# Values of eight key tiles behind every second section, units of 2 heads by 1024 queries, and tables for the places of scores and maxima

## The chip, the core and the metric

The kernel runs on one NeuronCore of a Trainium2 chip. The metric is the device time of one execution in microseconds (us). TensorE is called PE in the profile, VectorE DVE, ScalarE ACT, GpSimd POOL, and SyncE, which issues the DMAs here, SP. PEld is TensorE's weight load.

## The reference

One sequence of 2048 tokens of width 576. The output is the input plus an attention branch times a gated feed-forward branch, both of the layer-normed input:

```python
x = A_x                                  # (1, 2048, 576), float32
xn = _layernorm(x)
q, k, v = heads(xn @ wqkv)               # 32 heads of 18
p = softmax(q @ k.T * 18 ** -0.5)
s = (p @ v) @ wo
y = (gelu(xn @ w_gate) * (xn @ w_up)) @ w_down     # inner width 4608
return x + s * silu(y)
```

(heads() stands for the reshape and transpose of the original.)

## The kernel before

**Three phases.** A prologue norms x, projects it to q, k and v and writes them to DRAM. An epilogue projects the attention's output by wo and combines the branches. Between them lies the long middle, in which attention and the feed-forward part are interleaved; the change is there.

**Feed-forward.** The 2048 tokens are four blocks of 512 (`NB`), the inner width 4608 is 18 rounds of two groups of 128 (`NR`, `G`). One block and one group make a **section**, 144 in all: 27 pairs of matmuls (line 437), each pair two products of 64 rows of the contraction side by side, into one PSUM tile `pgu` that holds the gate and the up product (128x512 each). Each fp32 operand is split into a high and a low part (`wh`, `wl`), and three of the four products are taken, so a section is 9 chunks by 3 terms. Its 16th pair (index `SWAP` = 15) waits until the one before it is through, because the two halves change places there. After a section ScalarE takes the gelu of the gate (L452) and VectorE multiplies by the up part (L455). GpSimd then forms sums of the halves (`sums_a`, L472 to L477) and splits them (`cut_a`, L461 to L464) for the **down products** (`py`, L538), which come after every second section (`downs`): seven products by a fast scheme instead of eight, added into M by VectorE (L585). The w_down side of that scheme (T) is formed in the core for 18 rounds (`FORMED`: 13 of the first block, 5 of the second): GpSimd makes sums (`sums_b`), ScalarE writes the high parts (`high_b`, L511 to L514), GpSimd the low parts (`low_b`), and the result is stored. Other rounds load T from there in four pieces (`t_piece`).

**Attention.** It works in units (`NU` = 32) of four heads by 512 queries. Each unit sees 2048 keys as four chunks (`NA`) of 512. For a unit there are 32 score products `pe` (L901; 128 keys by 512 queries, two heads at once), whose exponentials ScalarE writes to SBUF as `pT` (L902), and 32 products `pm` (L860), the same scores the other way round, 128 queries by 512 keys, of which VectorE takes the largest (`mx`, L861). The maxima run 40 products ahead of the scores, so that each unit's maxima are known when its scores are made: `max_parts` reduces them (`neg`, L869), transposes (`mt`, L872), and writes a high and a low part (`mhl`, L874 on ScalarE, L875 on GpSimd), which DMAs put into two rows of the query tile. The product of keys and queries then has the maximum already subtracted. The **values stage** is the product of `pT` and the value tiles VS (`acc`, L918): for each of four key tiles and each of four heads 128 keys by 512 queries into 32 rows, in fp32. The first stage of a unit copies the result to `accs` (L922, ScalarE), later ones add to it (L924, VectorE).

**How they are woven.** The order of TensorE and of SP's queue is written out by hand, while a scheduler orders ScalarE, VectorE and GpSimd, except where `keep_in_program_order` holds two instructions. Eleven sections lead (`FIRST` gives how many maxima products each holds), then come 128 attention sections, then five in the epilogue (`ENDS`). An attention section carries eight scores and eight maxima, in turn (`SLOTS`). `spread` decides where they stand among the 27 pairs: by the formula i * 27 // 16 + 1, with the two nearest to SWAP moved to it. It also runs hooks at given pairs, such as the splits of the next weights. Behind each attention section come the values of its four key tiles, `max_parts` if a unit's maxima are complete, down products after every second one, and `finish`, which hands out the sums, the splits and the hooks of the next section.

All products of the middle take PSUM tiles of 128x1024 fp32 from one ring of four (`ring`). `pgu` holds its tile from the first pair of its section until gelu and multiplication have read it; a `pe` or `pm` tile comes free when its exponential or its reduction has read it. Tiles are taken in TensorE's order.

A key tile KA is held as two planes of 512 keys, one for each two of the four heads, seven chunks deep (`KB`).

Of the kernel before, what the change touches and what calls it, by code (L numbers as in the profile page):

```python
# [8 lines left out]
F32 = mybir.dt.float32  # L9
# [12 lines left out]
KT = 4  # L22
# [6 lines left out]
VW = QD * (DH + 1)  # L29
NQ = H // QD  # L30
NU = NQ * NB
# [3 lines left out]
VC = NT // NA  # L35
KB, VB = 7, 2
# [4 lines left out]
FIRST = (0, 0, 4, 5, 4, 5, 4, 5, 5, 4, 4)  # L41
# [4 lines left out]
SWAP = 3 * NK  # L46
DC, TH = D // 2, TB // 2
# [4 lines left out]
OTS = (4, 9, 0, 5)  # L52
# [37 lines left out]
def kernel(ctx: ExitStack, tc: tile.TileContext, x, wqkv, wo, w_gate, w_up, w_down, out):  # L90
# [11 lines left out]
    oT = dram.tile([NQ, P, S], F32, name="oT")  # L102
    rT = dram.tile([H, S], F32, name="rT")
# [297 lines left out]
    FF = {"w": ahead, "xd": XD, "down": [], "gates": [], "n": 0, "hooks": {}, "raw": {},  # L401
# [3 lines left out]
    KA = ffn.tile([P, 2 * KB, TB], F32R, name="KA")  # L405
    KS = [[KA[:, 2 * i + r] for r in range(2)] for i in range(KB)]
# [17 lines left out]
    def gate_up():  # L424
# [21 lines left out]
        return [lambda i=i: pair(i) for i in range(len(terms))], pg, pu  # L446

    def activate(pg, pu, g, n):

        h = ffn.tile([P, 3 + 3 * g, TH], F32, name=f"h{g}", bufs=2 - g)  # L450
        t1 = h[:, 0:2].rearrange("p a t -> p (a t)")
        nc.scalar.activation(t1, pg, AF.Gelu_apprx_tanh)  # L452
# [120 lines left out]
    def down(b, r, then={}):  # L573
# [16 lines left out]
        if FF["n"] < NF - ENDS:  # L590
# [35 lines left out]
    def section(specials=(), slots=False):  # L626
# [6 lines left out]
        pairs, pg, pu = gate_up()  # L633
        hooks, FF["hooks"] = FF["hooks"], {}
# [14 lines left out]
        if g == 0 and (b, r) in FORMED:  # L649
            raw = FF["rawd"]  # L650
            hook(12, lambda: sums_b(raw))
# [5 lines left out]
        for p in spread(pairs, specials, 1 if slots else None, hooks):  # L657
            p()
# [5 lines left out]
        FF["act"] = activate(pg, pu, g, n)  # L664
# [9 lines left out]

    def finish():
# [3 lines left out]
        g, h, s = n % G, FF["act"], part(b, r)  # L679
        pool, vec, act = nc.gpsimd, nc.vector, nc.scalar  # L680
        keep = tc.keep_in_program_order

        def hook(i, what):
            FF["hooks"].setdefault(i, []).append(what)

        parts = FF.pop("parts", False)

# [570 lines left out]
```

## Time and profile before

| | before |
|---|---|
| time, median of 3 runs | 2540.55 us (2539.89 to 2540.68) |
| the profiled execution's own time | 2539.57 us |
| its span in the profile | 2537.8 us |
| granted TensorE clock, mean | 0.999 |
| gate and up products (L437) | 36% of the chain that ended last |
| values (L918), down products (L538) | 18%, 16% |
| maxima, scores (L860, L901) | 10%, 9% |

The chain that ended last is followed back from the last instruction: at each step to what released it, or to the instruction before it on its engine. A group of instructions is given by line, engine and operation, what it writes and reads, the count, the busy time in all and the mean of one in ns, then the engine's idle time just before them and what ended most of it. A timeline row has the start from the span's begin, the time to the end, engine, line, operation, the tiles, and in brackets a wait and what ended it; rows of one kind that follow each other are drawn together, with their count. TensorE's matmuls are pipelined, so that durations overlap, and starts tell more than ends.

### The profile page before, as it was taken

The numbers are of one execution on the slowest core, as the hardware profiler recorded it, in microseconds if no ns is written. First come the engines' busy times: TensorE is split into PE (matmuls) and PEld (weight loads), VectorE is DVE, ScalarE is ACT, GpSimd is POOL, SyncE is SP. The second block draws the span as 40 slices with busy tenths as digits, with TensorE's granted clock in tenths as the row PEclk, the third lists the DMA queues.
The fourth block names the chain that finished last, engine by engine and source line by source line (L and its number), as shares of the span: only waits on it lengthen the run. The fifth ranks groups of instructions, "written<-read, shape, count | busy, mean of one in ns | idle before, by whom it ended". The sixth has DMA issues, their size and how long they took to land.

```text
span 2537.8 us, 59061 instructions
## 1 busy us (share of the span) xinstructions
PE 2529.8 (100%) x23434; PEld 1837.8 (72%) x23434; DVE 1891.7 (75%) x2085; ACT 1652.5 (65%) x1889; POOL 1587.1 (63%) x1652
## 2 busy tenths in 40 slices
PE   9999999999999999999999999999999999999999
PEld 8888866666766667666667766677666677666789
DVE  5326788888888888888887888888887788888247
ACT  3223377777777776666777666667777776777721
POOL 3005688787787775666657556566667565566772
PEclk9999999999999999999999999999999999999999
DMA  8855455555575556655666666656557666665666
GB/s 265 291 190 140 119 172 170 157 159 169 168 219 151 163 175 162 155 166 163 170 188 186 171 175 164 170 168 170 155 159 204 170 170 168 173 168 146 189 208 219
DMA packets 417419, 447.04 MB, mean 176 GB/s; under 512 B 114292, under 2 KB 294260, under 8 KB 417144
## 3 DMA queue, kind: packets, MB, share of 16 engines
q1 hardware_dynamic: 417144, 443.27, 60.3%
q8 instruction: 186, 3.05, 0.5%
q14 instruction: 89, 0.73, 0.1%
HBM read 345.99 MB, written 97.13 MB: 175 GB/s over the span
## 4 chain that ended last, share of the span: by engine, by line
PE 99%; DVE 1%; issue 0%; DMA 0%; ACT 0%; DVEq 0%
PE pgu L437 36%; PE acc L918 18%; PE py L538 16%; PE pm L860 10%; PE pe L901 9%; PE po L198 7%; PE po L1072 2%; PE py L598 1%; PE pt L268 0%; DVE ol L1055 0%; DMA xx<-in_A_x_dram 0%; DVE bs L227 0%; DVE xx L1088 0%; DVE yy L1062 0%; DVE M L1211 0%
## 5 line engine op out<-in xcount | busy, mean ns | idle before, releaser
L902 ACT ACTIVATE pT<-pe 128x1024 f32<-128x1024 f32 x1024 | 1034.8, 1026 | 490.6 <-PE pe L901 463.8
L861 DVE TENSOR_REDUCE mx<-pm 128x2 f32<-128x1024 f32 x1024 | 1219.5, 1226 | 155.2 <-PE pm L860 144.7
L437 PE MATMUL pgu<-xd,wh 64*128 64x512 f32 x5184 | 984.5, 393 | 0.4
L437 PEld LDWEIGHTS pgu<-xd,wh 64*128 64x128 f32 x5184 | 508.4, 184 | 126.4 <-issue 28.2
L120 POOL TENSOR_SCALAR wh<-raw 128x384 fp32r<-128x384 f32 x402 | 203.3, 517 | 598.7 <-PE pgu L437 487.7
L437 PE MATMUL pgu<-xd,wl 64*128 64x512 f32 x2592 | 519.4, 389 | 0.0
L918 PE MATMUL acc<-pT,VS 128*32 128x512 f32 x4096 | 466.0, 595 | 0.0
L860 PE MATMUL pm<-KA,QT 64*128 64x512 f32 x2048 | 424.3, 402 | 0.3 <-DVE mx L861 0.2
L901 PE MATMUL pe<-QT,KA 64*128 64x512 f32 x2048 | 413.6, 391 | 0.0
L122 POOL TENSOR_TENSOR wl<-raw,wh 128x384 fp32r<-128x384 f32 x402 | 402.7, 1016 | 12.1
L538 PE MATMUL py<-T,ah 64*128 64x288 f32 x3848 | 389.8, 294 | 0.0
L585 DVE TENSOR_TENSOR M<-py,M 128x576 f32<-128x576 f32 x448 | 333.3, 756 | 55.6 <-PE py L538 40.0
L538 PEld LDWEIGHTS py<-T,ah 64*128 64x128 f32 x3848 | 315.8, 184 | 53.2 <-issue 52.8
L464 POOL TENSOR_TENSOR al<-h,ah 128x512 fp32r<-128x512 f32 (+1 forms) x143 | 295.4, 2066 | 49.2 <-ACT ah L461 38.2
L918 PEld LDWEIGHTS acc<-pT,VS 128*32 128x32 f32 x4096 | 120.0, 109 | 276.8 <-issue 229.8
L538 PE MATMUL py<-T,al 64*128 64x288 f32 x1924 | 293.0, 291 | 0.0
L437 PEld LDWEIGHTS pgu<-xd,wl 64*128 64x128 f32 x2592 | 253.9, 185 | 37.0 <-POOL wl L127 0.3
L860 PEld LDWEIGHTS pm<-KA,QT 64*128 64x128 f32 x2048 | 201.4, 184 | 86.1 <-ACT pT L902 48.3
L901 PEld LDWEIGHTS pe<-QT,KA 64*128 64x128 f32 x2048 | 194.4, 184 | 86.7 <-DVE mx L861 12.6
L455 DVE TENSOR_TENSOR h<-h,pgu 128x512 f32<-128x512 f32 x139 | 95.6, 688 | 193.4 <-ACT h L452 188.6
L538 PEld LDWEIGHTS py<-T,al 64*128 64x128 f32 x1924 | 190.3, 185 | 0.0
L452 ACT ACT_TABLE_LOAD x129 | 165.5, 1283 | 2.3
(151 smaller groups left out, 2140.9 us busy)
## 6 DMA issues: line engine op xcount, KB each, us to landing
T<-ts SPq DMA_DIRECT2D x98, 576.0 KB
KA<-qk SPq DMA_DIRECT2D x768, 72.0 KB
T<-ts SPq DMA_DIRECT2D x98, 432.0 KB
raw<-in_B_w_up_dram SPq DMA_DIRECT2D x288, 128.0 KB
raw<-in_B_w_gate_dram SPq DMA_DIRECT2D x144, 160.0 KB
ts<-T SPq DMA_DIRECT2D x36, 576.0 KB
VS<-vs SPq DMA_DIRECT2D x128, 152.0 KB
qk<-t SPq DMA_DIRECT2D x72, 256.0 KB
```

Of the source, the lines that this page charges most:

```text
L120: first = nc.gpsimd.tensor_scalar(hi, raw, 1.0, 1.0, op0=ALU.mult, op1=ALU.mult)
L122: keep(nc.gpsimd.tensor_tensor(lo, raw, f(hi), op=ALU.subtract))
L198: nc.tensor.matmul(o, st, m, start=(i == 0), stop=(i == len(terms) - 1))
L437: one = nc.tensor.matmul((pg, pu)[half ^ x], w[1 + wp][c // XG][rr, c % XG, :], xd[k][xp][rr, :], start=(i == 0), stop=(i == len(terms) - 1))
L464: low = two.tensor_tensor(lo, raw, f(hi), op=ALU.subtract)
L538: one = nc.tensor.matmul(py[:, t, 0:DC], h[rr, a, t * P:(t + 1) * P], T[rr, w, k], start=x == 0 and n == 0, stop=x == 1 and n == len(terms ...
L585: nc.vector.tensor_tensor(M[:, m], py[:, :, 0:DC], M[:, m], op=ALU.add)
L860: nc.tensor.matmul(pm[:, a], QS[u, r][rr, t * P:(t + 1) * P], KS[(u * NA + c) % KB][r][rr, :], start=True, stop=True)
L861: nc.vector.tensor_reduce(MX[u][:, 2 * r:2 * r + 2, t, c], pm, axis=AX.X, op=ALU.max)
L901: nc.tensor.matmul(pe[:, a], KS[(u * NA + c) % KB][r][rr, t * P:(t + 1) * P], QS[u, r][rr, :], start=True, stop=True)
L902: nc.scalar.activation(PT[u, kt][:, 2 * r:2 * r + 2, :], pe, AF.Exp, scale=SCALE)
L918: nc.tensor.matmul(ACC[u][32 * a:32 * a + 32, :], VS[(u * NA + c) % VB][:, v:v + 32], pt[:, a, :], start=first, stop=last, skip_group_chec ...
```

## The change

**Units.** A unit is two heads by 1024 queries instead of four heads by 512. Both have four planes of 512 (head by query half); the counts of products and of sections stay. All planes now use the same two heads of a key chunk, so that KA has one plane per chunk, and a VS tile holds two heads. K and V loads have half the bytes; the query tile is loaded as two heads by 1024 columns.

**Values.** The values of eight key tiles (`RUN`) come behind every second section, just ahead of the down products, and `pT` has eight buffers. So two attention sections follow each other without anything between them on TensorE. A unit is copied once and added once to `accs` (lines 926 and 928 after).

**Gelu.** The first section of a round (g = 0) does not take a gelu: ScalarE copies both halves of `pgu` into `h0`. After the second section both gelus run, with one change of tables, then both multiplications. `sums_a` and `cut_a` of both sections follow in one `finish` of the round.

**Places.** `spread` takes the places of the specials of the two sections of a round from a table, `PLACES`, the first row for the first section. The index says before which of the 27 pairs a special stands.

**Formed rounds.** `high_b(0)` stays behind the values, `high_b(1)` is hooked to pair 8 of the next section, and the other hooks move.

**Ends.** Ten sections lead instead of eleven and six end instead of five; one more section, with its down product, stands behind the attention, and the attention's output is loaded into a tile of its own (OO).

```diff
-VW = QD * (DH + 1)
-NQ = H // QD
-NU = NQ * NB
+VW = 2 * (DH + 1)
+NQ = H // 2
+NU = NQ * S // (2 * TB)
...
+RUN = 2 * VC
...
-FIRST = (0, 0, 4, 5, 4, 5, 4, 5, 5, 4, 4)
+FIRST = (0, 0, 5, 5, 5, 5, 5, 5, 5, 5)
...
+PLACES = ((1, 2, 4, 5, 7, 8, 10, 11, 13, 15, 15, 17, 19, 20, 22, 23), (4, 5, 6, 8, 9, 11, 12, 13, 15, 15, 17, 18, 20, 22, 24, 25))
...
-    at = [-(-(i + 1) * n // m) - 1 if first is None else i * n // m + first for i in range(m)]
-    for i in sorted(range(m), key=lambda i: abs(at[i] - SWAP + 0.1))[:2]:
+    at = PLACES[first] if first is not None and m == 2 * SLOTS else [-(-(i + 1) * n // m) - 1 if first is None else i * n // m + first for i in range(m)]
+    for i in () if at in PLACES else sorted(range(m), key=lambda i: abs(at[i] - SWAP + 0.1))[:2]:
...
-    KA = ffn.tile([P, 2 * KB, TB], F32R, name="KA")
-    KS = [[KA[:, 2 * i + r] for r in range(2)] for i in range(KB)]
+    KA = ffn.tile([P, KB, TB], F32R, name="KA")
+    KS = [KA[:, i] for i in range(KB)]
...
+        if n in ATT and g == 0:
+            sums = bass.AP(h.tensor, h.offset, [list(h.ap[0]), [3 * TH, 2], [1, TB]])
+            keep(nc.scalar.activation(sums, two, AF.Copy))
+            return h
         if n in ATT:
-            tc.keep_in_program_order(nc.scalar.activation(one_exp[:, 1:2], one_exp[:, 0:1], AF.Exp))
+            keep(nc.scalar.activation(t1, pg, gelu))
+            h0 = FF["act"]
+            keep(nc.scalar.activation(flat(h0, 0), flat(h0, 0), gelu))
+            keep(nc.scalar.activation(one_exp[:, 1:2], one_exp[:, 0:1], AF.Exp))
+            nc.vector.tensor_tensor(t1, t1, pu, op=ALU.mult)
+            nc.vector.tensor_tensor(flat(h0, 0), flat(h0, 0), flat(h0, 3), op=ALU.mult)
+            return h0, h
+        nc.scalar.activation(t1, pg, gelu)
...
-        for p in spread(pairs, specials, 1 if slots else None, hooks):
+        for p in spread(pairs, specials, g if slots else None, hooks):
...
+        if (b, r + 1) in FORMED:
+            hook(15, lambda: load_rawd(part(b, r + 1)))
+        if (b, r) in FORMED:
+            high_b(0)
+            hook(8, lambda: high_b(1))
+            hook(2, lambda: low_b(0))
+            hook(11, lambda: low_b(1))
+            for k, i in enumerate((13, 20)):
+                hook(i, lambda k=k: t_piece(s, k, True))
+            for k, i in enumerate((2, 9)):
+                hook(i, lambda k=k: t_piece(s, 2 + k, True), True)
+        else:
+            t_piece(s, 0)
+            for k, i in ((1, 5), (2, 13), (3, 21)):
+                if n + 1 == ATT.stop:
+                    t_piece(s, k)
                 else:
-                    high_b(0)
-                    high_b(1)
-                hook(9 if lead else 2, lambda: low_b(0))
-                hook(16 if lead else 10, lambda: low_b(1))
-                for k, i in enumerate((19, 24) if lead else (1, 3) if late else (13, 20)):
-                    hook(i, lambda k=k: t_piece(s, k, True))
-                sums_a(g, h, vec if lead else pool)
-                hook(12, lambda: cut_a(0, h, pool, pool, keep))
-            else:
-                for k, i in enumerate((2, 9)):
-                    hook(i, lambda k=k: t_piece(s, 2 + k, True))
-                behind(lambda k: (sums_a(g, h, pool, k), cut_a(1, h, pool, pool, keep)))
-        else:
-            if g == 0:
-                for k, i in enumerate((None, 5, 27, 27) if late else (None, 5, 13, 21)):
-                    if i is None:
-                        t_piece(s, k)
-                    else:
-                        hook(i, lambda k=k: t_piece(s, k))
-            behind(lambda k: (sums_a(g, h, pool, k), cut_a(g, h, pool, pool, k)))
-        if g == G - 1:
-            FF["down"].append((b, r, n + 1))
+                    hook(i, lambda k=k: t_piece(s, k))
+        k = keep if FF.pop("parts", False) or (n + 1) % (NR * G) == 0 else lambda i: i
+        h0, h1 = FF["act"]
+        sums_a(0, h0, pool)
+        sums_a(1, h1, pool, k)
+        cut_a(0, h0, pool, pool, k)
+        cut_a(1, h1, pool, pool, k)
+        FF["down"].append((b, r, n + 1))
...
-                nc.tensor.matmul(pm[:, a], QS[u, r][rr, t * P:(t + 1) * P], KS[(u * NA + c) % KB][r][rr, :], start=True, stop=True)
+                nc.tensor.matmul(pm[:, a], QS[u, r][rr, t * P:(t + 1) * P], KS[(u * NA + c) % KB][rr, :], start=True, stop=True)
...
-                PT[u, kt] = att.tile([P, QD, TB], F32, name="pT", bufs=4)
+                PT[u, kt] = att.tile([P, QD, TB], F32, name="pT", tag="pT", bufs=RUN)
...
-            first, last = kt % VC == 0, kt % VC == VC - 1
+            first, last = kt % RUN == 0, kt % RUN == RUN - 1
...
-                v = t * VW + (DH + 1) * a
+                v = t * VW + (DH + 1) * (a % 2)
...
-            if last and kt < VC:
+            if last and kt < RUN:
...
-            for kt in range(i * SLOTS // 2, (i + 1) * SLOTS // 2):
-                values(u, kt)
             if im == 0 and um <= NU:
                 max_parts(um - 1)
-            load_v(n + 2)
+            if i % 2:
+                for kt in range((i - 1) * VC, (i + 1) * VC):
+                    values(u, kt)
+                load_v(n + 1)
+                load_v(n + 2)
             tasks(n, 1)
-            downs()
+            if i % 2:
+                downs()
             tasks(n, 2)
-            finish()
-            for b in range(2):
-                if n == NU * NA - NA + 2 * b:
-                    load_o(b)
+            if i % 2:
+                finish()
...
+        load_raw(FF["n"] + 2)
+        h, gelu = last_section()
+        todo.pop("rec")[0]()
+        down(NB - 1, NR - 4)
+        gelu()
+        for i in range(len(PIECES)):
+            t_piece(NR - 3, i)
+        sums_a(0, h, pool)
+        cut_a(0, h, pool, pool)
```

**The order.** The first place is TensorE around the end of a mid-kernel attention section. The numbers behind `xd` tell the section's operands; `pgu<-xd` are gate and up products, `pm<-KA,QT` maxima, `pe<-QT,KA` scores, `acc` values. Before, rows of the end of a first section, its values, and the start of the next:

```order
L437 MATMUL pgu<-xd_2_9475,wh 128x512 x2
L901 MATMUL pe<-QT_1963,KA 128x512 x2
L437 MATMUL pgu<-xd_3_9499,wh 128x512 x2
L437 MATMUL pgu<-xd_3_9499,wl 128x512 x2
L860 MATMUL pm<-KA,QT_1964 128x512 x2
L437 MATMUL pgu<-xd_3_9501,wh 128x512 x2
L918 MATMUL acc<-pT,VS_1937 32x512 x16
L437 MATMUL pgu<-xd_0_17946,wh 128x512 x2
L901 MATMUL pe<-QT_1963,KA 128x512 x2
L437 MATMUL pgu<-xd_0_17946,wl 128x512 x2
L860 MATMUL pm<-KA,QT_1964 128x512 x2
```

After, the same place on TensorE, the end of the first section of a round and the start of its second:

```order
L865 MATMUL pm<-KA,QT_1966 128x512 x2
L439 MATMUL pgu<-xd_2_17896,wh 128x512 x2
L439 MATMUL pgu<-xd_3_17922,wh 128x512 x2
L439 MATMUL pgu<-xd_3_17922,wl 128x512 x2
L439 MATMUL pgu<-xd_3_17924,wh 128x512 x2
L439 MATMUL pgu<-xd_0_17861,wh 128x512 x2
L439 MATMUL pgu<-xd_0_17861,wl 128x512 x2
L439 MATMUL pgu<-xd_0_17863,wh 128x512 x2
L439 MATMUL pgu<-xd_1_17876,wh 128x512 x2
L906 MATMUL pe<-QT_1965,KA 128x512 x2
L439 MATMUL pgu<-xd_1_17876,wl 128x512 x2
L865 MATMUL pm<-KA,QT_1967 128x512 x2
```

The last maxima product now stands five steps ahead of the border and not two, the values between the sections are gone, and the next section's first score stands behind four gate and up pairs instead of one.

The second place is TensorE within the second section of a round, where a maxima product's PSUM tile is needed again by the third special behind it. After (the first row is the section's first maxima product, the last the score that takes its tile):

```order
L865 MATMUL pm<-KA,QT_1967 128x512 x2
L439 MATMUL pgu<-xd_1_17878,wh 128x512 x2
L906 MATMUL pe<-QT_1965,KA 128x512 x2
L439 MATMUL pgu<-xd_2_17894,wh 128x512 x2
L439 MATMUL pgu<-xd_2_17894,wl 128x512 x2
L865 MATMUL pm<-KA,QT_1967 128x512 x2
L439 MATMUL pgu<-xd_2_17896,wh 128x512 x2
L906 MATMUL pe<-QT_1965,KA 128x512 x2
```

From the one to the other are seven pairs. By the formula of before the distance from a maxima product to that score is eight or nine pairs.

The third place is ScalarE around the end of a section in a round in which a unit's maxima are complete. `h` is the gelu's tile, `one_exp` a small exponential that calls the exponential's table back, `mhl` the maxima's high part. Before:

```order
L902 ACTIVATE pT<-pe 128x1024 x8
L452 ACT_TABLE_LOAD
L452 ACTIVATE h_18484<-pgu 128x512
L454 ACT_TABLE_LOAD
L454 ACTIVATE one_exp<-one_exp 128x1
L902 ACTIVATE pT<-pe 128x1024
L874 ACTIVATE mhl<-mt 128x32
L902 ACTIVATE pT<-pe 128x1024 x7
```

After, the same engine from the values of one round over both sections of the next (the second of three rows of `h` is the copy of both halves):

```order
L926 ACTIVATE accs<-acc 128x512
L907 ACTIVATE pT<-pe 128x1024 x8
L879 ACTIVATE mhl<-mt 128x32
L463 ACTIVATE h_18228<-pgu 128x2x512
L907 ACTIVATE pT<-pe 128x1024 x8
L466 ACT_TABLE_LOAD
L466 ACTIVATE h_18391<-pgu 128x512
L468 ACTIVATE h_18228<-h_18228 128x512
L469 ACT_TABLE_LOAD
L469 ACTIVATE one_exp<-one_exp 128x1
```

`mhl` moved from behind the next section's first exponential to ahead of the copy that empties `pgu`, and the gelu with its tables to behind the second section. In the formed rounds the three copies of `high_b`, in a row ahead of a section's eight exponentials before, are now one ahead of them and two behind the third.

More of the change, by code (lines that the diff above doesn't have):

```diff
@@ L571, in down_plain, with down @@
         halved(jobs)
-    def down(b, r, then={}):
+    def down(b, r, then={}, pairs=True):
         if b == 0 and r < PLAIN:
@@ L673, in downs, with lead_finish @@
             down(*FF["down"].pop(0)[:-1], then)
+    def lead_finish():
+        n = FF["n"] - 1
+        r, g = divmod(n, G)
+        if g == 1 and (0, r + 1) in NEXT:
+            load_rawd(r + 1)
+        if g == 0 and r > 0:
+            raw = FF["rawd"]
+            FF["hooks"].setdefault(4, []).append(lambda: cut_plain_b(raw))
+        cut_plain(g, FF["act"])
+        if g == G - 1:
+            FF["down"].append((0, r, n + 1))
     def finish():
@@ L972 @@
             downs()
-            finish()
+            lead_finish()
         scaled = gated = 0
@@ L1150 @@
         load_wo()
+        for b in range(2):
+            load_o(b)
         h, gelu = last_section()
-        todo.pop("rec")[0]()
         for k in range(2):
```

142 lines of the change are left out of this document (60 added, 82 removed).

## The prediction

> **What bounds the kernel now.** I read the page first: its busy times and the chain that ended last.
>
> ```profile
> span 2537.8 us, 59061 instructions
> PE 2529.8 (100%) x23434; PEld 1837.8 (72%) x23434; DVE 1891.7 (75%) x2085; ACT 1652.5 (65%) x1889; POOL 1587.1 (63%) x1652
> PE 99%; DVE 1%; issue 0%; DMA 0%; ACT 0%; DVEq 0%
> ```
>
> TensorE sets the end. Its busy time hides short waits, so from here on I go by when matmuls start. The next view is busy time by stage for one **round**: section, values, section, values, down products.
>
> ```profile
> core 0: us, PE busy (x) PEld busy (x) DVE busy (x) ACT busy (x) POOL busy (x), PEclk, DMA share, GB/s
> 1137.84:1148.05 10.21, 10.21 (x91) 8.06 (x87) 9.66 (x10) 7.87 (x8) 1.53 (x2) 1.00 1.02 248
> 1148.05:1151.62 3.57, 3.57 (x36) 0.94 (x34) 1.79 (x2) 3.51 (x5) 2.93 (x4) 1.00 0.71 202
> 1151.62:1161.83 10.21, 10.21 (x90) 7.79 (x86) 9.51 (x12) 8.03 (x10) 7.91 (x8) 1.00 0.38 106
> 1161.83:1165.40 3.57, 3.57 (x34) 0.94 (x32) 1.80 (x2) 3.51 (x5) 3.57 (x5) 1.00 0.47 140
> 1165.40:1171.00 5.60, 5.60 (x88) 5.58 (x86) 4.61 (x7) 0.09 (x1) 3.90 (x5) 1.00 0.69 172
> ```
>
> Inside a section VectorE is busy for 9.66 of 10.21 us; the values behind it are its rest, 1.79 of 3.57. TensorE hardly waits because that rest comes every 10 us. The change takes every second rest away, and packs the specials tighter.
>
> **Term 1: the borders that go.** Matmuls in time around one values stage (start, duration):
>
> ```profile
> 1147.25 0.39 PE L437 MATMUL pgu<-xd,wl 64*128 64x512 f32 x2
> 1147.48 0.40 PE L860 MATMUL pm<-KA,QT 64*128 64x512 f32 x2
> 1147.72 0.40 PE L437 MATMUL pgu<-xd,wh 64*128 64x512 f32 x2
> 1148.05 3.64 PE L918 MATMUL acc<-pT,VS 128*32 128x512 f32 x32
> 1151.62 0.51 PE L437 MATMUL pgu<-xd,wh 64*128 64x512 f32 x2
> 1151.95 0.40 PE L901 MATMUL pe<-QT,KA 64*128 64x512 f32 x2
> ```
>
> One pair of matmuls, which I call a **step**, takes 0.23 us from start to start (0.231 over a section of 43). The last before the values takes 0.33, the first behind them 0.33: 0.10 too much each. Inside the values stage:
>
> ```profile
> 1148.50 2.76 PE L918 MATMUL acc<-pT,VS 128*32 128x512 f32 x24
> ```
>
> Six of its eight groups of four: less one matmul of 0.61 these are 2.15 us for five gaps, 0.43 a group. Eight groups would be 3.43, and the stage took 3.57: 0.14 too much. A border thus costs 0.34 us in all, and 64 of 128 go: 64 x 0.342 = **-21.9 us**. Bounds: -9 (64 x 0.14, if a slow step shows up elsewhere instead) and -22; I take -21.9, since every slow step of the rows touches a border.
>
> The Trainium skill (TensorE: Matmul & The Clock Gate, LDWEIGHTS, and Part 3, The mechanism) says that a weight load takes its columns / 1.2 ns and hides behind running matmuls only where the row group differs. An estimate by that page: four loads of 32 columns going in and one of 128 coming out are exposed, 0.21 us a border, which would make this term -13.7 and the sum 2602. The rows here have 0.34 a border, and they decide.
>
> **Term 2: four PSUM places for a tighter row of work.** Each product is read out by one instruction:
>
> ```profile
> L902 ACT ACTIVATE pT<-pe 128x1024 f32<-128x1024 f32 x1024 | 1034.8, 1026 | 490.6 <-PE pe L901 463.8
> L861 DVE TENSOR_REDUCE mx<-pm 128x2 f32<-128x1024 f32 x1024 | 1219.5, 1226 | 155.2 <-PE pm L860 144.7
> ```
>
> A gate/up product holds one of the four places for its whole section. Three rotate, so each score (pe) or maxima (pm) product waits until the special three before it is read out. When a reader starts, and how it goes back to back:
>
> ```profile
> 1147.93 1.23 DVE L861 TENSOR_REDUCE mx<-pm 128x2 f32<-128x1024 f32 x1 [0.16 <-PE pm L860]
> ...
> 227.45 4.62 DVE L861 TENSOR_REDUCE mx<-pm 128x2 f32<-128x1024 f32 x4 [0.15 <-PE pm L860]
> ...
> 2365.27 2.86 ACT L902 ACTIVATE pT<-pe 128x1024 f32<-128x1024 f32 x3 [6.06 <-PE pe L901]
> ```
>
> The reduction starts 0.44 us after its product started (1147.48 to 1147.93, unrounded 0.441). Back to back, reductions come every (4.62 - 1.226) / 3 = 1.131 us, exponentials every (2.86 - 1.026) / 2 = 0.915. What a late place costs, the trace shows once in a section:
>
> ```profile
> 1143.25 0.41 PE L901 MATMUL pe<-QT,KA 64*128 64x512 f32 x2
> 1143.76 1.94 ACT L902 ACTIVATE pT<-pe 128x1024 f32<-128x1024 f32 x2 [0.42 <-PE pe L901]
> 1144.83 0.19 PEld L860 LDWEIGHTS pm<-KA,QT 64*128 64x128 f32 x2 [0.22 <-ACT pT L902]
> 1144.88 0.45 PE L860 MATMUL pm<-KA,QT 64*128 64x512 f32 x2
> 1145.17 0.39 PE L437 MATMUL pgu<-xd,wl 64*128 64x512 f32 x2
> ```
>
> The first of these two exponentials ends at 1143.76 + 1.026 = 1144.79, the weights load at 1144.83, and the step that began at 1144.88 lasts until 1145.17, 0.06 too long. So it really began at 1144.94, 0.157 after the place came free (unrounded). This exponential also started 0.06 later than others, 0.50 behind its product. The rule: a maxima product's place can be used again after 0.44 + 1.226 + 0.157 = 1.82 us, **7.9 steps**; a score's after 0.44 + 1.026 + 0.157 = 1.62, **7.0**, or 1.68 for one with the late start.
>
> Before, with the position in a section counted as pairs plus specials ahead, maxima stand at steps 3, 9, 14, 19, 24, 30, 35 and 41. A score comes 8 or 9 steps behind the maxima whose place it takes, and a single distance of 7 steps gives the 0.06 above: model and rows agree.
>
> After, in a first section, maxima stand at 3, 8, 13, 18, 24, 28, 33, 38, and the score at 25 takes the place of 18: seven steps, 1.62 us, where 1.82 are needed. It waits 0.21; with three times 0.008, 0.23. In a second section scores stand at 4, 8, 13, 18, 23, 27, 32, 38 and maxima at 6, 11, 16, 20, 24, 29, 35, 40. Each wait is the shortfall of its place less what was already waited in between: step 11 on 4, 0.07; 13 on 6, 0.21 - 0.07 = 0.14; 18 on 11, 0.07; 23 on 16, 0.14; 24 on 18 (six steps, 0.24 short), 0.10; 27 on 20, 0.11; 29 on 23 (six, 0.30 short), 0.09: together 0.71. A round waits 0.94 instead of 2 x 0.076. Of 64 rounds 61 have maxima, which run six sections ahead: 61 x 0.79 = **+48.3 us**. Lower bound: the place is free again 0.05 after its reader (when the weights load starts) and not 0.157; the same steps then give 0.10 + 0.41 a round, 61 x 0.50 = 30.7. I take 0.157, for it is measured at this very wait.
>
> **Term 3: ScalarE between two sections.** The copy of both halves of the gate/up product (128x1024, at the exponentials' 1.03) frees the place that step 8 of the second section takes. Ready 0.21 behind the border, it ends at 1.24, before 1.85 - 0.16: no wait. But in every second round the row of ScalarE has L874's small product ahead of that copy, and this hangs on the last reduction:
>
> ```profile
> 281.75 0.21 DVE L869 TENSOR_REDUCE neg<-mx 128x16 f32<-128x64 f32 x1
> 281.99 0.21 DVE L872 STREAM_TRANSPOSE mt<-neg 128x32 f32<-128x32 f32 x1
> 282.24 0.23 ACT L874 ACTIVATE mhl<-mt 128x32 fp32r<-128x32 f32 x1 [1.54 <-DVE mt L872]
> ```
>
> The last maxima product (step 38 of 43) is read out 0.51 us behind the border; 0.04 + 0.21 + 0.04 + 0.21 + 0.04 later ScalarE starts L874, at 1.04, and the copy at about 1.18. That ends at 2.21, and step 8 waits 2.21 + 0.16 - 1.85 = 0.52. Later ones shift: 0.22 + 0.21 + 0.24 + 0.06, in all 1.24 instead of 0.71. For 31 units: 31 x 0.53 = **+16.4 us**. Before, the same product stood behind an exponential of the next section, with 3.57 us of values between. Bounds: 0 (the copy comes first) and 0.65 x 31 = 20 (no part of the wait is shared); I take 16.4, as the rows of the order are plain.
>
> **Term 4: the 18 rounds that form w_down's sums.** Two of three copies move from the values stage to behind a first section's third exponential:
>
> ```profile
> L513 ACT ACTIVATE T<-tsum x18: 424/424/433, 313.0 to 904.8; 128x288 fp32r<-128x288 f32 x18
> L514 ACT ACTIVATE T<-rawd x18: 676/686/687, 313.4 to 905.7; 128x576 fp32r<-128x576 f32 x18
> ```
>
> They are 1.11 us alone and about 0.87 in a full queue (each laps by some 0.11, as 1.026 against 0.915). The third exponential ends at 4.01 us, so the fourth starts at 4.88, where its product (step 16) was ready at 4.14. It ends at 5.90, and the maxima product at step 24 waits 5.90 + 0.16 - 5.55 = 0.51. The 0.21 counted above then falls on step 31 instead, so 0.51 is added: 18 x 0.5 = **+9 us**, between 0 (the scheduler's order is not kept) and 12 (18 x 0.65).
>
> **Term 5: the end.** One section moves from the lead to behind the attention, and the down product behind it needs a w_down table, loaded during that one section of 27 x 0.231 = 6.2 us. Its loads, and the rate of the core's transfers in that part:
>
> ```profile
> T<-ts SPq DMA_DIRECT2D x98, 576.0 KB
> ...
> T<-ts SPq DMA_DIRECT2D x98, 432.0 KB
> 2422.90:2442.60 19.70, 19.51 (x163) 14.87 (x162) 10.43 (x10) 7.55 (x11) 11.31 (x12) 1.00 0.91 288
> ```
>
> Two of each are 2.06 MB, 7.2 us at 288 GB/s: 1 late, and some 1 for the landing: **+2 us** (0 to 6).
>
> **At nothing.** Half of the gelu's table loads go:
>
> ```profile
> L452 ACT ACT_TABLE_LOAD x129 | 165.5, 1283 | 2.3
> L463 POOL TENSOR_SCALAR ah<-h 128x1280 fp32r<-128x1280 f32 x65 | 82.3, 1267 | 5.7
> L464 POOL TENSOR_TENSOR al<-h,ah 128x1280 fp32r<-128x1280 f32 x66 | 195.5, 2963 | 9.0 <-ACT ah L461 3.6
> ```
>
> But they ran beside the values (ScalarE 3.51 of 3.57), where nobody waited for them. VectorE's additions to accs halve, beside the values too. K and V loads halve in bytes, and DMA holds 0% of the chain. GpSimd's sums and cuts come in one batch behind the second section; the last cut ends 1.27 + 2.96 us behind the down products as before, and the weights that it splits next are due in the section after, more than 10 us later. If that cover went, each late microsecond of a round would cost 64.
>
> **Sum**, against the profiled execution (2539.57 us, of which the span is 2537.8; the median 2540.55 lies 0.98 above it): 2539.6 - 21.9 + 48.3 + 16.4 + 9 + 2 = 2593.4. I say **2593**. With the lower bound of term 2 it is 2576, with term 1 at -9 it is 2606, with the upper ends of terms 3 to 5 it is 2604.
>
> **Rivals.**
> 1. *Faster: the borders alone.* The places come free in time, because one wait lets both readers catch up and none follows, or because readers of a tight row start earlier. Terms 2 to 4 then fall: 2539.6 - 21.9 + 2 = 2520. It decides at 0.34 us of added waits a round. For it:
>
> ```profile
> PEld pm L860 <- ACT pT L902: 48.3, 248, 0.5
> PEld acc L918 <- DVE mx L861: 45.3, 123, 0.4
> ```
>
> These are TensorE's two largest waits on its readers, under 100 us, and most of that is weight load that starts late behind running matmuls and costs nothing. Against it: seven steps are 1.62 us, and the reduction alone ends at 1.67.
> 2. *Only the rotation.* The copy comes first on ScalarE and the moved copies hide: 2539.6 - 21.9 + 48.3 + 2 = 2568, or 2550 with the lower bound of term 2.
> 3. *No change.* Added waits that just equal the 0.34 of a round: 2540.
>
> **Chances.** Forecast 0.70 (2570 to 2608); rival 2, 0.08; rival 1, 0.18; rival 3, 0.04. The range, 2518 to 2608, leaves out the lower half of rival 1 and a tenth above. About 0.2% is what this kernel's timing can tell from no change: faster 0.18, same 0.04, slower 0.78. The forecast's own range is 2570 to 2608.
>
> **What would show it.** Term 1: 64 values stages of 16 x 0.43 + 0.14 = 7.0 us, and 0.23 between the steps where two sections meet. Terms 2 and 3: first sections of 10.2 us, second ones of 10.6, or 11.2 where L874's product stands ahead of the copy; waits of pe on mx, few and short now, in hundreds of sections. Term 4: first sections of 10.7 us in 18 rounds. If second sections take 10.0 us, term 2 is wrong, and the time is near 2520.

## The result and the profile after

The changed kernel takes 2601.08 us (median of 4 runs, 2598.96 to 2601.92), the kernel before 2540.61 beside it: a ratio of 1.0237, 95% interval 1.022 to 1.0255. It is **slower by 60 us**; 2593 was forecast. The profiled execution took 2601.92 us.

The page of the changed kernel, busy times and the chain that ended last:

```profile
span 2600.1 us, 58832 instructions
PE 2576.2 (99%) x23476; PEld 1818.4 (70%) x23476; DVE 1847.8 (71%) x2013; ACT 1531.8 (59%) x1758; POOL 1601.1 (62%) x1665
PE 89%; DVE 4%; ACT 3%; DMA 2%; issue 1%; POOL 1%; SPq 0%; POOLq 0%; DVEq 0%; ACTq 0%
```

VectorE and ScalarE do 44 and 121 us less than before, and yet they hold 4% and 3% of the chain now, where they held 1% and 0%. The busy share of TensorE still says 99%, which shows how little it tells of short waits.

Busy time by stage, two rounds in mid-kernel, each stretch from one stage's first matmul to the next one's (first section, second section, values, down products, then both sections of the next round):

```profile
core 0: us, PE busy (x) PEld busy (x) DVE busy (x) ACT busy (x) POOL busy (x), PEclk, DMA share, GB/s
1154.64:1164.93 10.29, 10.29 (x90) 7.74 (x88) 10.14 (x10) 8.21 (x8) 5.72 (x4) 1.00 0.81 245
1164.93:1176.23 11.30, 11.05 (x89) 7.45 (x85) 9.73 (x12) 8.91 (x10) 5.94 (x8) 1.00 0.30 86
1176.23:1183.23 7.00, 7.00 (x66) 1.97 (x64) 2.34 (x3) 4.11 (x6) 6.21 (x8) 1.00 0.45 119
1183.23:1188.86 5.63, 5.63 (x88) 5.63 (x86) 4.65 (x7) 0.00 (x0) 1.98 (x3) 1.00 0.37 96
1188.86:1199.06 10.20, 10.20 (x90) 7.51 (x88) 10.04 (x10) 8.21 (x8) 5.71 (x4) 1.00 0.81 247
1199.06:1209.84 10.78, 10.78 (x89) 7.39 (x85) 9.17 (x9) 8.91 (x9) 5.73 (x7) 1.00 0.31 88
```

The values stage takes the 7.0 us that term 1 worked out, and the second sections take 11.30 with mhl and 10.78 without, where 11.2 and 10.6 were forecast. Over all 61 rounds with maxima the two sections take 21.49 us together on the mean, 20.44 before: 61 x 1.047 = 63.9 more; the 64 values stages take 7.004 instead of 2 x 3.571, 8.8 less. That is 55.1 of the 62.4 us between the two profiled executions. (Means over the rounds, here and below, are taken from the starts of TensorE's matmuls: by stage, or step by step, where a step is 0.23 us long if nothing waits.)

TensorE's waits, in all, times, longest (the view of waits; first the changed kernel, then, of the kernel before, the one row that the prediction spoke of without showing it):

```profile
PEld pm L865 <- ACT pT L907: 85.0, 362, 0.6
PEld pe L906 <- DVE mx L866: 79.7, 276, 0.4
PEld pe L906 <- ACT h L463: 21.5, 31, 0.9
```

```profile
PEld pe L901 <- DVE mx L861: 12.6, 76, 0.2
```

Scores wait for maxima's places 276 times instead of 76, and 31 times, once per unit, for the copy of pgu.

The step at which the copy comes late, in the second section from 1164.93 on (a timeline):

```profile
1165.49 0.22 DVE L874 TENSOR_REDUCE neg<-mx 128x16 f32<-128x64 f32 x1
1165.75 0.21 DVE L877 STREAM_TRANSPOSE mt<-neg 128x32 f32<-128x32 f32 x1
...
1165.99 0.23 ACT L879 ACTIVATE mhl<-mt 128x32 fp32r<-128x32 f32 x1 [1.20 <-DMA KA<-qk]
1166.13 1.01 ACT L463 ACTIVATE h<-pgu 128x1024 f32<-128x1024 f32 x1
...
1167.19 0.19 PEld L906 LDWEIGHTS pe<-QT,KA 64*128 64x128 f32 x2 [0.69 <-ACT h L463]
```

mhl starts 1.06 us behind the border (1.04 in the prediction), the copy at 1.20 (1.18), and the score's weights load 0.05 us after it ends. ScalarE stands idle for 1.20 us ahead of mhl, while the copy that TensorE needs is queued behind it. The profile puts that idle time down to a DMA; mhl reads mt, which was written at 1165.96.

And a first section in a formed round, the copies behind the third exponential:

```profile
610.92 0.43 ACT L532 ACTIVATE T<-tsum 128x288 fp32r<-128x288 f32 x1
...
611.25 0.67 ACT L533 ACTIVATE T<-rawd 128x576 fp32r<-128x576 f32 x1
...
611.82 2.86 ACT L907 ACTIVATE pT<-pe 128x1024 f32<-128x1024 f32 x3
...
612.89 0.19 PEld L865 LDWEIGHTS pm<-KA,QT 64*128 64x128 f32 x2 [0.58 <-ACT pT L907]
```

The fourth exponential starts 0.90 us after the first copy (0.87 in the prediction).

### The profile page after: what moved, and what is told of

The parts are those of the page before. It is cut to its first block, busy times and chain, and to the rows that moved or that the text cites. A ratio compares the mean times of both kernels' runs of the same rounds, so it can differ in the third digit from the quotient of the medians.

```text
span 2600.1 us, 58832 instructions
## 1 busy us (share of the span) xinstructions
PE 2576.2 (99%) x23476; PEld 1818.4 (70%) x23476; DVE 1847.8 (71%) x2013; ACT 1531.8 (59%) x1758; POOL 1601.1 (62%) x1665
## 4 chain that ended last, share of the span: by engine, by line
PE 89%; DVE 4%; ACT 3%; DMA 2%; issue 1%; POOL 1%; SPq 0%; POOLq 0%; DVEq 0%; ACTq 0%
PE pgu L439 28%; PE acc L922 17%; PE py L557 15%; PE pe L906 10%; PE pm L865 9%; PE po L200 7%; DVE mx L866 3%; PE po L1080 1%; ACT h L463 1%; ACT pT L907 1%; DMA od<-rT 0%; PE py L617 0%; ACT T L533 0%; DMA raw<-in_B_w_up_dram 0%; DMA KA<-qk 0%
## 5 line engine op out<-in xcount | busy, mean ns | idle before, releaser
L439 PE MATMUL pgu<-xd,wh 64*128 64x512 f32 x5184 | 909.2, 390 | 1.0 <-POOL wh L122 0.5
L604 DVE TENSOR_TENSOR M<-py,M 128x576 f32<-128x576 f32 x448 | 332.8, 756 | 171.9 <-PE py L557 161.3
L922 PE MATMUL acc<-pT,VS 128*32 128x512 f32 x4096 | 452.7, 594 | 0.0
L906 PE MATMUL pe<-QT,KA 64*128 64x512 f32 x2048 | 437.0, 415 | 7.8 <-ACT h L463 7.8
L865 PE MATMUL pm<-KA,QT 64*128 64x512 f32 x2048 | 434.8, 414 | 3.6 <-ACT pT L907 1.4
L124 POOL TENSOR_TENSOR wl<-raw,wh 128x384 fp32r<-128x384 f32 x405 | 406.6, 1017 | 10.6
L557 PE MATMUL py<-T,ah 64*128 64x288 f32 x3904 | 395.7, 294 | 0.2
L557 PEld LDWEIGHTS py<-T,ah 64*128 64x128 f32 x3904 | 319.9, 184 | 55.1 <-issue 53.6
L922 PEld LDWEIGHTS acc<-pT,VS 128*32 128x32 f32 x4096 | 126.6, 110 | 291.7 <-issue 263.6
L865 PEld LDWEIGHTS pm<-KA,QT 64*128 64x128 f32 x2048 | 195.4, 183 | 132.7 <-ACT pT L907 85.0
L482 POOL TENSOR_SCALAR ah<-h 128x512 fp32r<-128x512 f32 (+1 forms) x132 | 123.8, 938 | 181.6 <-PE py L557 181.2
L470 DVE TENSOR_TENSOR h<-h,pgu 128x512 f32<-128x512 f32 x64 | 44.0, 687 | 124.1 <-ACT h L466 124.1
```

The costliest lines, as they stand in the source:

```text
L124: keep(nc.gpsimd.tensor_tensor(lo, raw, f(hi), op=ALU.subtract))
L439: one = nc.tensor.matmul((pg, pu)[half ^ x], w[1 + wp][c // XG][rr, c % XG, :], xd[k][xp][rr, :], start=(i == 0), stop=(i == len(terms) - 1))
L557: one = nc.tensor.matmul(py[:, t, 0:DC], h[rr, a, t * P:(t + 1) * P], T[rr, w, k], start=x == 0 and n == 0, stop=x == 1 and n == len(terms ...
L604: nc.vector.tensor_tensor(M[:, m], py[:, :, 0:DC], M[:, m], op=ALU.add)
L865: nc.tensor.matmul(pm[:, a], QS[u, r][rr, t * P:(t + 1) * P], KS[(u * NA + c) % KB][rr, :], start=True, stop=True)
L906: nc.tensor.matmul(pe[:, a], KS[(u * NA + c) % KB][rr, t * P:(t + 1) * P], QS[u, r][rr, :], start=True, stop=True)
```

## The experiments

Two theories. **Rotation**, that of the prediction: a PSUM place is needed again before its reader is through, and two pieces of ScalarE's work stand in the way; nothing else in the rounds costs. **Missing rest**: the readers fall behind because the values stage, in which they caught up, now comes half as often. The kernel before ran beside each, at 2540.2 to 2540.9 us.

| run | median us | expected by rotation | ratio to before, 95% interval |
|---|---|---|---|
| before_places | 2595.25 | 2589 to 2600 | 1.0216 (1.020 to 1.0231) |
| formula | 2580.56 | 2582 | 1.0158 (1.0143 to 1.0173) |
| eight | 2558.18 | 2563 | 1.0069 (1.0053 to 1.0086) |
| half_max | 2553.90 | 2560 | 1.0053 (1.0038 to 1.0068) |
| mhl_pool | 2581.74 | 2585 | 1.0163 (1.0149 to 1.0176) |
| high_pool | 2591.95 | 2592 | 1.0207 (1.0191 to 1.0223) |
| all3 | 2555.54 | 2528 | 1.0061 (1.0049 to 1.0074) |
| all3_split | 2570.62 | all3 + 21.9 | 1.0118 (1.0104 to 1.0132) |
| late_start | 2531.90 | 2532 | 0.9964 (0.9951 to 0.9976) |
| late_start_split | 2545.94 | late_start + 15 to 22 | 1.0021 (1.0012 to 1.003) |
| late_start_end | 2538.34 | 2529 | 0.9992 (0.9983 to 1.0001) |
| late_start_loads | 2539.03 | 2530 to 2532 | 0.9995 (0.9986 to 1.0004) |

**before_places**: the kernel before, with the table.

```diff
 SWAP = 3 * NK
+PLACES = ((1, 2, 4, 5, 7, 8, 10, 11, 13, 15, 15, 17, 19, 20, 22, 23), (4, 5, 6, 8, 9, 11, 12, 13, 15, 15, 17, 18, 20, 22, 24, 25))
...
-        for p in spread(pairs, specials, 1 if slots else None, hooks):
+        for p in spread(pairs, specials, g if slots else None, hooks):
```

> The kernel before, with the change's table of places and nothing else: values stages still stand behind every section. Theory 'rotation' (a place is needed again too soon, wherever the rests lie): 0.23 to 0.41 us of waits in first sections, 0.71 in second ones, where there were 0.076: 61 rounds x 0.80 to 0.97, so 2589 to 2600 us. Rival 'missing rest' (the readers fall behind because the values no longer come between): nothing is missing here, so 2540 to 2550 us.

Two sections of one round, with a values stage behind each:

```profile
1160.77:1171.54 10.77, 10.77 (x91) 7.35 (x87) 9.88 (x10) 7.87 (x8) 1.53 (x2) 1.00 1.00 258
1175.11:1185.62 10.51, 10.51 (x91) 7.46 (x87) 10.18 (x12) 8.64 (x11) 8.21 (x8) 1.00 0.35 97
```

Both were 10.21 before. The first has the table's second row (here the down products come behind the values of a round's first section) and is 0.56 us longer, the other 0.30. Every rest is in its place, and the 55 us are lost all the same: the table alone loses them, and the missing rest falls as the main cause.

**formula**: the changed kernel with the places of before.

```diff
-    at = PLACES[first] if first is not None and m == 2 * SLOTS else [-(-(i + 1) * n // m) - 1 if first is None else i * n // m + first for i in range(m)]
-    for i in () if at in PLACES else sorted(range(m), key=lambda i: abs(at[i] - SWAP + 0.1))[:2]:
+    at = [-(-(i + 1) * n // m) - 1 if first is None else i * n // m + 1 for i in range(m)]
+    for i in sorted(range(m), key=lambda i: abs(at[i] - SWAP + 0.1))[:2]:
```

> The changed kernel with the places of before (the formula, for both sections). Rotation: the tight steps go, but the first score now stands behind one gate/up pair, before the copy of pgu has given its place back: second sections wait about 0.7 us in rounds without mhl and 1.0 with it, all rounds together 64 us of waits instead of 83, so about 2582. Rival 'missing rest': at least 2601. If the table of places were the whole loss: 2520.

First sections fell to 10.05 us where nothing is formed, but second ones took 10.87 and, with mhl, 11.02 (means over the rounds): their steps 0 to 3 alone lost some 0.7, waiting for the copy. So the table has a use, the late first score, but pays for it with steps that are too tight.

**eight**: the changed kernel with another table.

```diff
+PLACES = ((0, 0, 2, 4, 5, 6, 9, 10, 13, 15, 15, 18, 20, 20, 23, 24), (1, 3, 5, 7, 8, 10, 12, 13, 15, 16, 18, 19, 22, 22, 25, 27))
...
         out.append(pairs[i])
-    return out
+    return out + [p for p, j in zip(specials, at) if j == n]
```

> The changed kernel with another table of places, in which a maxima product's place is needed again after 8 steps or more and a score's after 7 or more, and the first score of a second section is late enough for the copy. Rotation: first sections 0.02 us of waits, second ones 0.12 (that of the 16th pair), 1.3 where mhl is ahead of the copy; 45 us in all rounds instead of 83, so 2563. Missing rest: 2601, as VectorE and ScalarE have the same work between the same values stages.

43 us less with the same work between the same stages, which speaks against the missing rest. That the time came out near the forecast is luck, though, for the waits lie elsewhere. First sections took 10.44 us and lost some 0.45 at steps 1 to 4, where 0.02 was expected; second ones with mhl took 10.44, 0.22 more than those without, where 1.2 more were expected. The two errors cancel; **all3** below finds the first. **half_max** shortens the reader instead:

```diff
-            nc.vector.tensor_reduce(MX[u][:, 2 * r:2 * r + 2, t, c], pm, axis=AX.X, op=ALU.max)
+            nc.vector.tensor_reduce(MX[u][:, 2 * r:2 * r + 2, t, c], pm[:, :, 0:TB // 2], axis=AX.X, op=ALU.max)
```

> The changed kernel, its reductions reading only the first 256 of each 512 keys (half of the maxima's work is left out). Rotation: a maxima product's place is free 0.44 + 0.69 + 0.157 = 1.29 us after its start instead of 1.82 (0.69 from VectorE's 128x512 addition), so all waits of scores on maxima go and those of maxima on scores (six steps) stay: 41 us in all rounds instead of 83, so 2560. If the waits hung on something else than the reductions: 2601.

47 us less. Its waits of TensorE show which half is left:

```profile
PEld pm L865 <- ACT pT L907: 115.2, 465, 1.1
PEld pm L865 <- DVE M L604: 11.3, 57, 0.2
PEld pe L906 <- ACT h L463: 4.6, 26, 0.4
```

No row of scores that wait for maxima is left, and the other half has grown from 85.0 to 115.2: those waits were in part covered. By itself this run does not tell the theories apart, since it also takes work from VectorE, which would help against a missing rest too; before_places and eight do.

**mhl_pool** and **high_pool** take one piece of ScalarE's work each to GpSimd:

```diff
-            nc.scalar.activation(hl[:, 0], mt, AF.Copy)
+            nc.gpsimd.tensor_scalar(hl[:, 0], mt, 1.0, 1.0, op0=ALU.mult, op1=ALU.mult)
```

> The changed kernel, the high part of the maxima (mhl) written by GpSimd instead of ScalarE, so that the copy of pgu follows a first section's last exponential at once. By term 3 second sections of rounds with mhl go from 11.31 to 10.75 us: 30 x 0.53, so 2585. If the copy were late for another reason: 2601.

```diff
-            keep(nc.scalar.activation(T[:, 0, 2], t[:, 0], AF.Copy))
-            keep(nc.scalar.activation(T[:, 0, 0:2], q[:, 0:4:3], AF.Copy))
+            keep(nc.gpsimd.tensor_scalar(T[:, 0, 2], t[:, 0], 1.0, 1.0, op0=ALU.mult, op1=ALU.mult))
+            keep(nc.gpsimd.tensor_scalar(T[:, 0, 0:2], q[:, 0:4:3], 1.0, 1.0, op0=ALU.mult, op1=ALU.mult))
```

> The changed kernel, the two copies of high_b(1) by GpSimd instead of ScalarE. By term 4 first sections of formed rounds go from 10.70 to 10.29 us or somewhat less: 18 x 0.5, so 2592. If these copies are hidden: 2601.

They give 19.3 and 9.1 us. Second sections of rounds with mhl went from 11.31 to 10.78 on the mean, first sections of formed rounds from 10.73 to 10.33: terms 3 and 4 are shown, at about their size.

**all3**: eight, mhl_pool and high_pool together.

> The changed kernel with the other table of places (8 steps), mhl and high_b(1) by GpSimd. If terms 2 to 4 are all of the waits in the rounds: 10 us of waits are left of 83, so 2528, which is below the kernel before by 12. If a rest is missing in double sections: 2560 or more.

A miss by 27 us. In eight, and so here, little of terms 3 and 4 was left to win: first sections that form took 10.44 us there, as the others did, and a second section lost 0.22 to mhl. And TensorE at the start of a first section loses time:

```profile
1165.31 1.42 DVE L604 TENSOR_TENSOR M<-py,M 128x576 f32<-128x576 f32 x2
1165.50 0.39 PE L906 MATMUL pe<-QT,KA 64*128 64x512 f32 x2
...
1165.72 0.40 PE L865 MATMUL pm<-KA,QT 64*128 64x512 f32 x2
...
1166.21 0.50 PE L439 MATMUL pgu<-xd,wh 64*128 64x512 f32 x2
1166.51 0.43 PE L439 MATMUL pgu<-xd,wl 64*128 64x512 f32 x2
...
1166.78 0.19 PEld L906 LDWEIGHTS pe<-QT,KA 64*128 64x128 f32 x2 [0.28 <-DVE M L604]
```

The new table puts a score and a maxima product ahead of the first gate/up pair, which stands at step 2 (1166.21), and the second score at step 4 (1166.78). These two take the places of the last two down products, which VectorE is still adding to M (0.756 us each, one behind the other) 1.2 us into the section: the first of the two additions ends at 1166.06, 0.15 before the pair starts, the second at 1166.73, 0.05 before the score's weights load. From step 1 to step 5 some 0.45 us are lost, in each of 61 rounds, 27 us. That is not a rest that is missing but a third user of the ring, which the table was laid out without.

**late_start** has yet another table, with mhl and high_b(1) by GpSimd as in all3. A gate/up pair comes first, and the products that take those two places are now the first maxima product, at step 4, and the second score, at step 7; most other places move by a pair or two:

```diff
+PLACES = ((1, 3, 5, 6, 8, 9, 11, 12, 15, 15, 17, 19, 20, 22, 24, 24), (2, 4, 5, 7, 9, 10, 12, 13, 15, 16, 18, 19, 21, 22, 26, 26))
```

> As all3, but first sections start their second and third special two steps later (places 1, 3, 5, ... instead of 0, 0, 2, ...), so that the last two down products have been added to M when their PSUM places are needed. The 0.45 us that all3's first sections lost at steps 1 to 4 goes, and one wait of 0.07 comes in second sections: 2555.5 - 61 x 0.38, some 2532, below the kernel before (2540.6). If the missing rest were behind all3's loss, it moves elsewhere: 2550 or more.

```profile
1154.46:1164.46 10.00, 10.00 (x90) 7.43 (x88) 9.68 (x10) 7.78 (x8) 5.71 (x4) 1.00 0.84 252
1164.46:1174.71 10.25, 10.25 (x89) 7.58 (x87) 9.34 (x9) 8.59 (x10) 5.72 (x7) 1.00 0.34 96
```

2531.90 us, as expected, and the fastest of all: 0.36% below the kernel before. The two sections of this round go through in 20.25 us without a rest between, and in 20.36 on the mean of the 61.

**all3_split** and **late_start_split** put the borders back (`pT` keeps its eight buffers):

```diff
-RUN = 2 * VC
+RUN = VC
...
-            if i % 2:
-                for kt in range((i - 1) * VC, (i + 1) * VC):
-                    values(u, kt)
-                load_v(n + 1)
-                load_v(n + 2)
+            for kt in range(i * VC, (i + 1) * VC):
+                values(u, kt)
+            load_v(n + 2)
...
```

> As all3, but with the values of four key tiles behind every section again: 64 more borders. Term 1 (0.342 us a border, no wait left to hide it): 21.9 above all3, some 2550. By the Trainium skill's figures (TensorE: Matmul & The Clock Gate, LDWEIGHTS): 0.21 a border, 13.7 above all3. If a border costs nothing or gives back a rest: level with all3 or below it.

> As late_start, with values of four key tiles behind every section again, 64 more borders. Gross 0.342 us a border by term 1; all3_split stood 0.24 above all3, since rests hide some 0.1 of waits: 15 to 22 us above late_start, 2547 to 2554. By the Trainium skill's figures 13.7 above.

15.1 and 14.0 us, 0.24 and 0.22 for each of 64 borders. Step by step a border still costs what term 1 says: in late_start_split, on the mean, 0.098 too much at the last step before the values, 0.105 at the first behind them, and 3.571 twice instead of 7.004, together 0.34. Against that the sections of late_start lose 0.08 more a round at other steps, waits that the values' rest would hide. So the rest does exist, and is worth 0.08 us a round, not 0.79. Up to the end of the last values stage the borders of late_start_split thus cost 16.5 us, 0.26 each. It wins 2.75 back behind that stage, from where it takes 135.64 us to the end and late_start 138.39. Of these, 1.5 are the moved section's down product, which in late_start waits 1.24 us for its table (T, at 2405.75) and in late_start_split does not.

**late_start_end** tried to win back some of term 5.

```diff
-        load_wo()
-        for b in range(2):
-            load_o(b)
+        load_raw(first + 3)
+        load_o(0)
+        load_wo()
+        load_o(1)
         h, gelu = last_section()
...
-        load_raw(first + 3)
...
-                pool.tensor_tensor(wl[rr, i], t[rr], f(wh)[rr, i], op=SUB)
+                (vec if i % 2 else pool).tensor_tensor(wl[rr, i], t[rr], f(wh)[rr, i], op=SUB)
```

> As late_start, with three edits behind the attention: the weights of the last sections are loaded ahead of wo and the attention's output, only one of its two loads stands ahead of wo, and VectorE takes two of GpSimd's five subtractions for wo's low part. By term 5's account (5.8 us of added waits behind the last values, of which 1.4 on weights loaded late and 1.3 on wo's low part) 2 to 4 us below late_start, some 2529. If these waits are given back at the next place: level with late_start.

6.4 us slower. A down product of the epilogue stands still:

```profile
2433.46 1.30 DVE L1043 TENSOR_TENSOR wol<-xx,woh 128x576 fp32r<-128x576 f32 x1 [1.09 <-ACT woh L1041]
2435.74 1.35 DVE L1043 TENSOR_TENSOR wol<-yy,woh 128x576 fp32r<-128x576 f32 x1 [0.98 <-ACT woh L1041]
2437.01 2.07 DVE L604 TENSOR_TENSOR M<-py,M 128x576 f32<-128x576 f32 x3
...
2437.81 0.50 PEld L617 LDWEIGHTS py<-T,ah 128*128 128x128 f32 x2 [4.56 <-DVE M L604]
```

VectorE's additions of the down products are queued behind two subtractions that wait for wo. I took the moved subtractions for the cause, and **late_start_loads** is the run without them:

> As late_start_end without its third edit: the loads are moved, and GpSimd keeps all five subtractions for wo's low part. If late_start_end lost its 6 us because VectorE's additions of the down products stood behind subtractions that wait for wo: level with late_start or up to 2 us below it, 2530 to 2532. If the moved loads alone did it (wo comes later): 2536 or more.

2539.03: that theory fell, or rather is not enough. The additions now run (L604 from 2433.11 on), but the wait comes back at another place:

```profile
2445.77 1.29 POOL L771 TENSOR_TENSOR on<-on,od 128x512 f32<-128x512 f32 x1 [4.54 <-DMA od<-rT]
...
2454.90 0.50 PE L439 MATMUL pgu<-xd,wh 64*128 64x512 f32 x2 [3.92 <-POOL wh L122]
```

With the loads moved, the five pieces of wo come to ScalarE from 2432.98 to 2437.28, in late_start from 2431.26 to some 2433.6, and GpSimd's subtractions end 2.1 us later (2441.22). More is lost behind them: GpSimd then waits for the load `od<-rT`, 4.54 us instead of 1.31, which stands behind the moved ones in SP's queue and is issued at 2436.03 instead of 2427.68. The split of the next weights starts behind that, 5.6 us later than in late_start. The order of the loads is what costs; which of the moved loads does, was not tried.

## Why the prediction was right, and where it was off

- **What bounds the kernel**: right. TensorE sets the end, and what changes the time is the start of its matmuls, not its busy share. One sentence there is wrong: that TensorE hardly waits because a rest comes every 10 us. before_places has every rest and loses 55 us, and late_start has half of them and loses 0.08 us a round by it. The distances in the row of work are what kept the waits small before.
- **Term 1 (-21.9)**: right in size at the steps (7.004 us for the stage, 0.34 a border); net of the waits that a border hides it is 0.26 a border, 16.5 in all, in late_start_split. The estimate by the Trainium skill's figures (TensorE: Matmul & The Clock Gate, LDWEIGHTS) was 13.7; the whole difference of 14.0 between late_start_split and late_start lies there, but not for that reason, since the steps at the border itself lose 0.34 and not 0.21. That the sum by these figures, 2602, comes nearer to 2601 than 2593 does is luck too, for what the sum lacked lies elsewhere (below).
- **Term 2 (+48.3)**: right, in mechanism and place. First sections that form nothing lose 0.21 at steps 24 and 25 (0.21 on the score at 25 in the prediction), second ones without mhl 0.13 up to step 12 (0.07 at 11), then 0.10 at 13, 0.07 by 20, 0.14 by 23, 0.05 at 24, 0.15 by 27 and 0.09 at 29: 0.73, against 0.71. (Maxima run five sections ahead, 40 products at eight a section, and not six; 61 whole rounds have them all the same, and the first section of one more.) before_places moves the waits, at nearly the same steps, into the kernel before and loses 55 us; eight, half_max and late_start take them away in three ways.
- **Term 3 (+16.4)**: right. 11.31 against 10.79 on the mean, and 19.3 us back in mhl_pool. The waits stand where they were forecast: 0.54 at step 8, then 0.22, 0.21, 0.23 and 0.07, against 0.52, 0.22, 0.21, 0.24 and 0.06.
- **Term 4 (+9)**: right. 0.4 a round in the trace, 9.1 us back in high_pool.
- **Term 5 (+2)**: the mechanism was too narrow. From the last values stage to the end the changed kernel takes 138.63 us and the one before 120.63. The moved section and its down product are 27 x 0.231 + 0.34 (the wait at SWAP) + 5.63 = 12.2 of the 18.0; 5.8 are added waits. The table's load was a small part of them; the rows of TensorE's waits there say what else:

```profile
2493.45 0.50 PE L439 MATMUL pgu<-xd,wh 64*128 64x512 f32 x2 [0.46 <-POOL wh L122]
2494.53 0.49 PE L439 MATMUL pgu<-xd,wl 64*128 64x512 f32 x2 [0.58 <-POOL wl L124]
2503.27 0.53 PE L617 MATMUL py<-T,ah 128*128 128x288 f32 x2 [0.38 <-DVE h L1143]
2510.56 0.40 PE L1080 MATMUL po<-wol,oo 128*128 128x288 f32 x1 [1.14 <-POOL wol L1043]
```

GpSimd has the last section's sums and cuts, the splits of weights and wo's low part in one queue, and the weights and wo's low part are now a little late for TensorE. The term counted one load and left that queue out. But these four rows hold 2.6 of the 5.8 us, and that the queue is the cause is read from them and not shown: late_start_end, which took two subtractions out of it, moved loads as well, and lost time.
- **At nothing**: right for the tables, the additions to accs, K and V: the 121 us that ScalarE does less show as a gain at no step of the rounds.
- The rivals: the places do not come free in time, and the copy does not come first. The sum was 53.8 us above the profiled execution of before, and the changed kernel's is 62.4 above it. Of the 8.5 that are missing 3.8 are term 5 and 3.3 the rounds with maxima and the values; the last 1.4 lies outside them and was not taken apart.

## What to carry to other kernels

Where tiles of PSUM rotate, work out for each the time from the product's start until its place can be written again, in units of the row of work, and check each distance of a new order against it. Here 1.82 us against 1.62 cost some 50 us in a kernel whose readers were busy for 71% and 59%. Count every user of the ring, the stage before too. And look at what an in-order engine has queued ahead of the one instruction that gives a place back: 0.2 us of work that waits for data can cost 0.5.

## What the runs showed of the hardware

A stall costs more than its length. In late_start_loads TensorE waited 3.9 us at 2450.98, and the granted clock (the column behind POOL's) was half afterwards:

```profile
2440.00:2450.00 10.00, 8.85 (x67) 8.72 (x66) 1.93 (x3) 1.26 (x2) 4.49 (x4) 1.00 0.92 228
...
2456.50:2461.80 5.30, 5.30 (x28) 3.94 (x24) 0.95 (x1) 0.00 (x0) 5.05 (x7) 0.50 0.81 299
2461.80:2468.00 6.20, 6.13 (x54) 4.71 (x52) 0.00 (x0) 0.00 (x0) 5.86 (x8) 0.98 0.30 78
```

The steps took 0.426 us instead of 0.231 for 12 steps, 2.3 us on top of the wait. That, with the wait, is most of the 7 us by which this run lies above late_start. In late_start_end it is the same: TensorE's matmuls stop for 4.33 us until 2437.81, and from 2437.80 to 2440.00 the granted clock is 0.50. The Trainium skill (TensorE: Matmul & The Clock Gate, Part 1: The HAM clock gate) says that the array falls to half its clock after an idle window of about 3.4 us and comes back after one that is busy; these rows agree, as far as two waits of 3.9 and 4.3 us can tell. One of 1.24 us in late_start left the clock at 1.00. The waits in the changed kernel's rounds, half a microsecond each and less, lowered no clock: 1.00 in all six rows of its stages.
